# The issue order of four engines set by a table

## The chip, the core and the metric

The kernel runs on one core of one Trainium2 chip. The metric is device time in microseconds (us) from the start to the end of one execution. The core has TensorE (PE in the profile; PEld are its weight loads), VectorE (DVE), ScalarE (ACT), GpSimd (POOL) and SyncE (SP), each with its own queue of instructions, and 16 DMA engines. In this kernel SyncE does nothing but issue DMAs; its rows in the trace are named SPq.

## The reference

Linear attention with a random feature map, then two feed-forward layers. Batch 4, 8 heads, 576 positions, head dimension 64, 128 features; 2304 tokens of 512 elements go through the layers.

```python
def phi(x):
    proj = np.einsum('bhsd,md->bhsm', x, omega)
    sq = np.sum(x * x, axis=-1, keepdims=True) / 2.0
    h = proj - sq
    h = h - np.max(h, axis=-1, keepdims=True)
    return np.exp(h) / np.sqrt(m)
q_p, k_p = (phi(q_s), phi(k_s))
kv = np.einsum('bhsm,bhsd->bhmd', k_p, v)
z = np.sum(k_p, axis=2)
num = np.einsum('bhsm,bhmd->bhsd', q_p, kv)
den = np.einsum('bhsm,bhm->bhs', q_p, z)[..., None] + 1e-06
x = num / den                                  # then as (2304, 512)
h = x @ w_in                                   # 512 -> 2048
x = (h * (1.0 / (1.0 + np.exp(-1.702 * h)))) @ w_out
out = ((x @ w_a) * (x @ w_b)) @ w_out2         # 512 -> 1536 -> 512
```

Inputs are float32. The kernel works with pairs of float16, a high and a low part, so that each product takes three matmuls (high by high, high by low, low by high).

## The kernel before

**Stages.** The attention of batch 0 comes first (0 to about 57 us). Then the first feed-forward layer, ffn1, runs tile by tile, 512 tokens each, one tile for each batch and a rest tile of 256 tokens (L1134); beside ffn1 of one batch, the attention of the next batches is computed (batch 1 from 57 us on, batches 2 and 3 up to about 400 us). From about 500 us on ffn2 computes the second layer with a scheme of seven products for each block of 2x2 (`product`, L814 to L816 for a and b, `o_step`, L910 to L912 for the last matrix); its sums on VectorE are L835 (`total`), L841 (`times`), L864 and L868 (`ab_forms`), L918.

**Attention of one pair of heads** (`features`, in `kphase32` and `qphase`): load (`a_load`, L348, L352), high and low part (L403 on ScalarE, L404 on VectorE), a transpose by DMA (L409, xt), squares on ScalarE (L423, L431), the projection on TensorE (L415, L416), the maximum (L481), bias (L487), exponentials (L447), their parts (L457, L458), then for k the product with v (L529 to L531), for q a second DMA transpose (L575, eqT), products with kv (L585) and the division (L594 to L599). The result goes by a DMA transpose to xT (L635), in batch 0 by TensorE with the split L624.

**ffn1** (L655 to L692): for each of 16 blocks f of the hidden layer, h = w_in by xT on TensorE (L655 to L657), an activation on ScalarE (L664), th on VectorE (L667), gh on ScalarE (L676) and gl on VectorE (L677), then four accumulations y on TensorE (L690 to L692).

**Weights.** The weights come in 34 chunks of 1 MB (16 for w_in and w_out; then w_a0, w_b0, w_o2_0, w_a1, w_b1 and so on, two chunks each). Each is loaded as `wraw` (L201 in `w_load`, two buffers) and made into two float16 parts in `w_ops`: L215, L255 and L263 on VectorE assemble `wf` (128x1024 each), for the second layer L249 makes four sums `sx`, L273 on ScalarE gives the high part and L222 on VectorE the low part. A load i waits until L263 of chunk i-2 has read its buffer. `w_steps` takes so many steps of this generator at a point of the program, `w_need` as many as a use of the weights asks for.

**What sets the order.** The program is written as generators that are stepped in turn (`run`, `side_step`). The order of each engine's instructions comes from a scheduler that works while the program is built, with the order in which the program was written as a base. In five places a tie, `with tc.issue_after(x)`, keeps what is issued inside from going ahead of x: `fill` in ffn2 behind the last product (L971), the weight steps in `run` behind the last bias (L1077), the loads of v (L1090), the loads of k for the batch after (L1108) behind the transposed features of a q, and the first eight weight steps behind those of q0_2 (L1198).

Of the kernel before, what the change touches and what calls it, by code (L numbers as in the profile page):

```python
# [2 lines left out]

# [25 lines left out]
S_Y = 2.0**10  # L29
S_AB = 2.0**18  # L30
SILU = 3


@with_exitstack
def fused_kernel(
# [13 lines left out]
    nc = tc.nc  # L49
    B, H, S, D = q.shape  # L50
    M = omega.shape[0]
    DM, F1 = w_in_d.shape
    F2 = w_a_d.shape[1]
    P = 128
# [7 lines left out]
    T = 2 * NT + 1  # L62
# [5 lines left out]
    XSC = 1.0 / S_X  # L68
    DEN_EPS = 1e-6 * M / S_X

    mp = ctx.enter_context(tc.tile_pool(name="mp", bufs=4))
    stg = ctx.enter_context(tc.tile_pool(name="stg", bufs=2))
    ydram = ctx.enter_context(tc.tile_pool(name="ydram", bufs=1, space=bass.MemoryType.DRAM))
# [229 lines left out]
    own = {}  # L303
# [341 lines left out]
    def ffn1(j, xh, xl, n):  # L645
# [13 lines left out]
        def h_unit(f, cs=range(KC)):  # L659
            h_products(f, cs)  # L660
            ph = phs.pop(f)
            th = mp.tile([P, 512], F32, tag="f32", name=f"th{j}_{f}")
            if j < SILU:
                nc.scalar.activation(  # L664
# [67 lines left out]
    def y_load(j, n):  # L732
        yfs[j] = late["pool"].tile([P, KC, 512], F32, tag="yf", name=f"yf{j}", bufs=1)
        nc.sync.dma_start(out=yfs[j][:, :, :n], in_=ys[j][:, :, :n])
# [39 lines left out]
    def form_load(s, n):  # L774
        fo = form_tile(s)
        nc.sync.dma_start(out=fo[:, :, :, :, : n // 2], in_=stored[s % NT2])
# [15 lines left out]
    def ffn2():  # L792
# [8 lines left out]
        def product(k, m):  # L801
            g, j, n, nm = groups[k]
            b, a, r, fresh = PRODUCTS[m]
            if fresh:
                pool, tag = TAGS[b]
                banks[k, b] = pool.tile([P, 512], F32, tag=tag, name=f"p{nm}{b}{g}_{j}")
            o, w, fo = view(banks[k, b], n), w_ab[nm, g], forms[k // 2]
            h = n // 2
            for i in range(2):
                for c in range(2):  # L810
                    wh, wl = w[:, 0, i, a, c], w[:, 1, i, a, c]
                    xh, xl = fo[:, 0, r, c, :h], fo[:, 1, r, c, :h]
                    first, final = fresh and i == 0 and c == 0, i == 1 and c == 1
                    nc.tensor.matmul(o[:, i], wh, xh, start=first, stop=False, skip_group_check=True)  # L814
                    nc.tensor.matmul(o[:, i], wh, xl, start=False, stop=False, skip_group_check=True)  # L815
                    own["pe"] = nc.tensor.matmul(  # L816
                        o[:, i], wl, xh, start=False, stop=final, skip_group_check=True
                    ).ins
# [27 lines left out]
        def last(k):  # L846
            g, j, n, nm = groups[k]
            if nm == "a":
                nc.scalar.copy(sums[k][:, 3, :n], banks[k, "A"][:, :n])
                return  # L850
            times(k, slice(3, 4), banks[k, "A"][:, None, :n])
            side.append(ab_forms(k))
# [80 lines left out]
        def fill():  # L933
            if todo:
                o_step()
# [20 lines left out]
        def step(k, i):  # L956
            convert(k, i)
            step_side()
# [6 lines left out]
        for k, (g, j, n, nm) in enumerate(groups):  # L965
            s = k // 2
            if k:
                product(k - 1, 4)
                last(k - 1)
            if n < SM and nm == "a":  # L970
                with tc.issue_after(own["pe"]):  # L971
                    fill()
            if nm == "a" and s + 1 < NG * NT2:
                nj, nn = tiles[(s + 1) % NT2]
                if s + 1 < NT2:
                    y_load(nj, nn)
                else:
                    form_load(s + 1, nn)
            if nm == "b" and s + 1 < NT2:
                side.append(y_forms(*tiles[s + 1]))  # L980
            end = k == len(groups) - 1
            step(k, 0)
            product(k, 5)
            keep(k, 5)
            if nm == "b" and not end:
                fill()
            step(k, 1)
            product(k, 6)
            keep(k, 6)
            if nm == "b" and not end:  # L990
                fill()
            step(k, 2)
            product(k, 2)
            total(k, "B", 1, 0)
            if nm == "b":
                fill()
            step(k, 3)
            product(k, 3)
            total(k, "C", 6, 1)
            if nm == "b" and not end:  # L1000
                fill()
            step(k, 4)
            product(k, 7)
            total(k, "A", 5, 2)
            if nm == "b":
                times(k, slice(0, 3), sums[k][:, :, :n])
            if nm == "a" or j < B - 1:
                fill()
            step(k, 5)
            if nm == "a":  # L1010
                finish()
                fill()
            elif not end:
                while len(todo) > (j == B - 1):
                    o_step()
            begin(k + 1)
            if nm == "b":
                finish()
# [52 lines left out]
    def run(gen, rate, wmax):  # L1071

        due = 0.0
        for _ in gen:
            due += rate
            if rate < 1:
                with tc.issue_after(own["nb"]):  # L1077
                    w_steps(int(due), wmax)
            else:
                w_steps(int(due), wmax)  # L1080
            due -= int(due)
            side_step()
# [4 lines left out]

    def v_parts(b, behind):
        for part in range(NT):
            with tc.issue_after(behind.ins):  # L1090
                v_load(b, part)
            yield

# [8 lines left out]
    def begin_q(b, pool, xT, psp, t0, lag, f32):  # L1102
        for hp in range(NHP):
            def nx(hp=hp):
                if hp + 1 < NHP:
                    a_load(pool, "q", b, hp + 1)
                if b:
                    with tc.issue_after(own["xt", f"q{b}_{hp}"].ins):  # L1108
                        a_load(pool, "k", b + 1, hp)
                if hp + 1 == NHP:  # L1110
                    begin(b + 1, 0, v_parts(b + 1, own["xt", f"q{b}_{hp}"]))

            begin(b, t0 + lag * hp, qphase(pool, b, hp, xT, psp, nx, f32))
# [55 lines left out]
    with tc.tile_pool(name="att", bufs=2) as att:  # L1169
        own["om"] = att.tile([P, D], F32, tag="om", name="om", bufs=1)  # L1170
        nc.scalar.dma_start(out=own["om"], in_=omega)
        a_load(att, "k", 0, 0)
        a_load(att, "k", 0, 1, nc.scalar)
        zero = att.tile([P, 2, P], F16, tag="zero", name="zero", bufs=1)
        nc.vector.memset(zero, 0.0)
        for _ in range(10):
            nc.tensor.matmul(idle[:, 0:256], zero[:, 0], zero.rearrange("p a b -> p (a b)"), start=True, stop=True)
        warm = att.tile([P, 1], F32, tag="warm", name="warm", bufs=1)
        nc.vector.memset(warm, 0.0)
        nc.scalar.activation(out=warm, in_=warm, func=AF.Exp)  # L1180
        alloc_own(att)
        prep(att)
        fillers(5)
        for hp in range(2, NHP):
            a_load(att, "k", 0, hp)
        w_steps(START_W, NW1)
        begin_k(0, att, psp_start, 0, LAG, True)
        begin_q(0, att, xT, psp_start, NHP * LAG, LAG, True)
        for n in range(VT):
            side_step()  # L1190
        v_load(0)
        finish_side(0)
        fillers(FILL)
        w_load(0)
        w_load(1)
        for hp in range(NHP):
            a_load(att, "k", 1, hp)
        with tc.issue_after(own["xt", "q0_2"].ins):  # L1198
            w_steps(POST_W, NW1)
        following.append(ffn1(0, *xparts(xT), SM))  # L1200
        for b in range(1, B):
            x1 = x_tile(b, zp, "z")
            t0 = (0, 0, 1, -EARLY)[b]
            if b < 3:
                begin_k(b, att, psp_att, t0, AL, b == 1)
            begin_q(b, att, x1, psp_att, t0 + NHP * AL, AL, b == 1)
            if b == 2:
                begin_k(3, att, psp_att, 37 - EARLY, AL, False)
            ahead = next_tile(b, lambda: ffn1(b, *xparts(x1), SM))
            if b == 1:  # L1210
                run(head(following[0], 3), 1, NW1)
                run(following[0][0](first=3), 1, NW1)
                ahead()
            else:
                if b == 2:
                    run(head(following[-1], 3), 11 / 32, NW1 + 2)
                run(following[-1][0](ahead, 3 if b == 2 else 2), 11 / 32, (NW1 + 2, NWE)[b - 2])
# [11 lines left out]
    first.close()  # L1229
    late["sums"] = ctx.enter_context(tc.tile_pool(name="sums", bufs=1, side="right", reuse_waits="tile"))  # L1230
    ffn2()


# [34 lines left out]
```

## Time and profile before

| | |
|---|---|
| median of 3 runs | 897.08 us (896.01 to 898.03) |
| span of the profiled execution | 897.5 us |
| TensorE busy | 874.1 us (97%), weight loads 628.0 us |
| VectorE busy | 674.2 us (75%) |
| ScalarE busy | 457.6 us (51%) |
| instructions on TensorE, VectorE, ScalarE, GpSimd | 7094, 1212, 1088, 10 |
| DMA | 105.35 MB, 117 GB/s on average |

The page gives no time of the profiled execution apart from its span, from the first to the last instruction. That span is 0.4 us above the median. The rows below come from the trace of this execution; times are in us from its start.

### The profile page before, as it was taken

The numbers are of one execution on the slowest core, as the hardware profiler recorded it, in microseconds if no ns is written. First come the engines' busy times: TensorE is split into PE (matmuls) and PEld (weight loads), VectorE is DVE, ScalarE is ACT, GpSimd is POOL, SyncE is SP. The second block draws the span as 40 slices with busy tenths as digits, with TensorE's granted clock in tenths as the row PEclk, the third lists the DMA queues.
The fourth block names the chain that finished last, engine by engine and source line by source line (L and its number), as shares of the span: only waits on it lengthen the run. The fifth ranks groups of instructions, "written<-read, shape, count | busy, mean of one in ns | idle before, by whom it ended". The sixth has DMA issues, their size and how long they took to land.

```text
span 897.5 us, 17366 instructions
## 1 busy us (share of the span) xinstructions
PE 874.1 (97%) x7094; PEld 628.0 (70%) x7094; DVE 674.2 (75%) x1212; ACT 457.6 (51%) x1088; POOL 1.4 (0%) x10
## 2 busy tenths in 40 slices
PE   8999999999999999999999999999999999999997
PEld 6874655645554455444448888888888889888886
DVE  4889999787797787999611179987999557566766
ACT  6777875677656775564323354544443122233221
POOL 0000000000000000000000000000000000000000
PEclk8999999999999999999999999999999999999999
DMA  6945886344674314785401045232332022223312
GB/s 174 251 143 163 223 209 218 95 124 92 129 172 118 74 28 80 136 269 223 141 1 48 16 138 175 108 89 83 130 130 81 3 42 85 83 95 129 77 49 71
DMA packets 129343, 105.35 MB, mean 117 GB/s; under 512 B 97776, under 2 KB 111088, under 8 KB 127216
## 3 DMA queue, kind: packets, MB, share of 16 engines
q1 hardware_dynamic: 128558, 103.66, 41.0%
q8 instruction: 55, 0.90, 0.4%
q10 hardware_dynamic: 706, 0.59, 0.2%
q14 instruction: 24, 0.20, 0.1%
HBM read 71.07 MB, written 17.69 MB: 99 GB/s over the span
## 4 chain that ended last, share of the span: by engine, by line
PE 66%; DVE 17%; ACT 7%; DMA 4%; issue 2%; ACTq 0%; SPq 0%
PE y L690 4%; PE ph L655 4%; PE ph L656 4%; PE y L691 4%; PE ph L657 4%; PE y L692 4%; DMA xt_k<-x_k 3%; PE oA L912 2%; PE oA L910 2%; PE pbA L816 2%; PE pbA L814 2%; PE pbA L815 2%; PE oA L911 2%; PE pa L569 2%; PE paA L814 2%; PE paA L816 2%
## 5 line engine op out<-in xcount | busy, mean ns | idle before, releaser
L691 PE MATMUL y<-gl,w_out 128*128 128x512 f16 (+1 forms) x320 | 114.4, 358 | 0.6 <-DVE gl L677 0.4
L692 PE MATMUL y<-gh,w_out 128*128 128x512 f16 (+1 forms) x320 | 114.3, 358 | 0.0
L690 PE MATMUL y<-gh,w_out 128*128 128x512 f16 (+1 forms) x320 | 112.3, 358 | 0.7 <-ACT gh L676 0.7
L677 DVE SCALAR_TENSOR_TENSOR gl<-th,gh 128x512 f16<-128x512 f32 (+1 forms) x80 | 50.7, 635 | 66.6 <-ACT gh L676 66.3
L655 PE MATMUL ph<-xT,w_in 128*128 128x512 f16 x256 | 97.0, 379 | 1.5 <-DMA xT<-x_q_3x 0.7
L656 PE MATMUL ph<-xT,w_in 128*128 128x512 f16 x256 | 97.0, 379 | 0.3 <-DVE xT L624 0.3
L657 PE MATMUL ph<-xT,w_in 128*128 128x512 f16 x256 | 97.0, 379 | 0.0
L814 PE MATMUL paA<-forms,w_a 128*128 128x256 f16 (+1 forms) x240 | 61.0, 262 | 1.6 <-DVE ca L835 1.3
L814 PE MATMUL pbA<-forms,w_b 128*128 128x256 f16 (+1 forms) x240 | 61.0, 262 | 0.7 <-DVE cb L835 0.7
L816 PE MATMUL pbA<-forms,w_b 128*128 128x256 f16 (+1 forms) x240 | 61.0, 262 | 0.0
L815 PE MATMUL pbA<-forms,w_b 128*128 128x256 f16 (+1 forms) x240 | 61.0, 262 | 0.0
L816 PE MATMUL paA<-forms,w_a 128*128 128x256 f16 (+1 forms) x240 | 61.0, 262 | 0.0
L815 PE MATMUL paA<-forms,w_a 128*128 128x256 f16 (+1 forms) x240 | 61.0, 262 | 0.0
L912 PE MATMUL oA<-w_o,ab 128*128 128x256 f16 x216 | 58.9, 273 | 0.6 <-DVE ab L868 0.5
L910 PE MATMUL oA<-w_o,ab 128*128 128x256 f16 x216 | 58.9, 273 | 0.1
L911 PE MATMUL oA<-w_o,ab 128*128 128x256 f16 x216 | 58.9, 273 | 0.0
L676 ACT ACTIVATE gh<-th 128x512 f16<-128x512 f32 (+1 forms) x80 | 47.1, 589 | 23.0 <-DVE th L667 22.0
L824 ACT COPY ka<-paA 128x512 f32<-128x512 f32 (+1 forms) x30 | 16.3, 544 | 82.1 <-PE paA L816 82.1
L918 DVE SCALAR_TENSOR_TENSOR o<-oA,o 128x512 f32<-128x512 f32 (+1 forms) x45 | 28.4, 633 | 33.6 <-PE oA L912 33.6
L692 PEld LDWEIGHTS <-w_out 128*128 128x128 f16 x320 | 31.4, 98 | 29.3 <-issue 1.9
L657 PEld LDWEIGHTS <-w_in 128*128 128x128 f16 x320 | 31.5, 98 | 28.7 <-DVE w_in L222 1.1
L690 PEld LDWEIGHTS <-w_out 128*128 128x128 f16 x320 | 31.5, 99 | 28.6 <-issue 1.2
(211 smaller groups left out, 2373.8 us busy)
## 6 DMA issues: line engine op xcount, KB each, us to landing
wraw<-in_moe_w_out_dram SPq DMA_DIRECT2D x14, 1024.0 KB
forms<-fd SPq DMA_DIRECT2D x8, 1792.0 KB
wraw<-in_moe_w_in_dram SPq DMA_DIRECT2D x8, 1024.0 KB
fd<-forms SPq DMA_DIRECT2D x4, 1792.0 KB
wraw<-in_moe_w_a_dram SPq DMA_DIRECT2D x6, 1024.0 KB
wraw<-in_moe_w_b_dram SPq DMA_DIRECT2D x6, 1024.0 KB
vt<-in_v_dram SPq DMA_DIRECT2D x16, 256.0 KB
rawq<-in_q_dram SPq DMA_DIRECT2D x16, 256.0 KB
```

The source lines that it names most:

```text
L655: nc.tensor.matmul(ph[:, :n], w[:, 0, c, fs], xh(c), start=(c == 0), stop=False)
L656: nc.tensor.matmul(ph[:, :n], w[:, 0, c, fs], xl(c), start=False, stop=False)
L657: nc.tensor.matmul(ph[:, :n], w[:, 1, c, fs], xh(c), start=False, stop=(c == KC - 1))
L690: nc.tensor.matmul(o, w[:, 0, f % 4, cs], gh[f][:, :n], start=(f == 0), stop=False)
L691: nc.tensor.matmul(o, w[:, 0, f % 4, cs], gl[f][:, :n], start=False, stop=False)
L692: nc.tensor.matmul(o, w[:, 1, f % 4, cs], gh[f][:, :n], start=False, stop=(f == FC1 - 1))
L814: nc.tensor.matmul(o[:, i], wh, xh, start=first, stop=False, skip_group_check=True)
L815: nc.tensor.matmul(o[:, i], wh, xl, start=False, stop=False, skip_group_check=True)
L816: own["pe"] = nc.tensor.matmul(o[:, i], wl, xh, start=False, stop=final, skip_group_check=True).ins
L910: nc.tensor.matmul(bank[:, t], lh, wh, start=first, stop=False, skip_group_check=True)
L911: nc.tensor.matmul(bank[:, t], lh, wl, start=False, stop=False, skip_group_check=True)
L912: nc.tensor.matmul(bank[:, t], ll, wh, start=False, stop=final, skip_group_check=True)
```

## The change

The five ties become `contextlib.nullcontext`. At the end of the program a table is unpacked that holds, for each of four engines (TensorE, ScalarE, VectorE, SyncE), a permutation of that engine's instructions: 6870, 1019, 1212 and 224 numbers, each the place of an instruction in the order in which the program issues it. Between any two that follow one another in the table an edge is added without a semaphore (`NoSync`). The edges chain each engine's queue to one order. Instructions, operands, buffers and data dependencies remain as they are; GpSimd is not in the table.

Against the order of the kernel before, 1972 of TensorE's 6870 positions differ, 1687 of them between 50 and 400 us, by at most 90 places; 683 of ScalarE's, 841 of VectorE's (up to 254 places earlier, 45 later) and 120 of SyncE's.

```diff
+import contextlib
...
+ORDER = (
+    "eNqt3buua9uyGNZf2bjxCdjrRVKZASsXYMCJoMBwpMROBCeG/12ztyLn2ufeK8OBgz2x15ocfIxeg4tsVb3q//6X//Qf/+U//PWf"
...
+)
...
+    no_tie = contextlib.nullcontext
...
             if n < SM and nm == "a":
-                with tc.issue_after(own["pe"]):
+                with no_tie():
                     fill()
...
             if rate < 1:
-                with tc.issue_after(own["nb"]):
+                with no_tie():
                     w_steps(int(due), wmax)
...
         for part in range(NT):
-            with tc.issue_after(behind.ins):
+            with no_tie():
                 v_load(b, part)
...
                 if b:
-                    with tc.issue_after(own["xt", f"q{b}_{hp}"].ins):
+                    with no_tie():
                         a_load(pool, "k", b + 1, hp)
...
-        with tc.issue_after(own["xt", "q0_2"].ins):
+        with no_tie():
             w_steps(POST_W, NW1)
...
     ffn2()
+    import base64, json, zlib
+    nosync = mybir.DependencyInfo(mybir.DependencyClass.NoSync, mybir.DependencyReason.DATA)
+    for name, order in json.loads(zlib.decompress(base64.b64decode(ORDER))).items():
+        engine = getattr(mybir.EngineType, name)
+        ins = [i for i in nc.cur_bb.bb.instructions if i.engine == engine and type(i).__name__ != "BassTilePoolBoundary"]
+        assert len(ins) == len(order), (name, len(ins), len(order))
+        for a, b in zip(order, order[1:]):
+            tc.add_manual_dep(ins[b], ins[a].name, nosync, reason="order")
```

## Rows read from the trace of the kernel before

**Rows 1.** The page's engine line: busy us, share of the span, instructions
```profile
PE 874.1 (97%) x7094; PEld 628.0 (70%) x7094; DVE 674.2 (75%) x1212; ACT 457.6 (51%) x1088; POOL 1.4 (0%) x10
```

**Rows 2.** Windows: stretch, length, busy us of each engine, granted clock, DMA share, GB/s
```profile
57.00:82.00 25.00, 22.47 (x129) 11.18 (x129) 24.80 (x42) 17.02 (x64) 0.00 (x0) 1.00 0.57 163
82.00:160.00 78.00, 77.28 (x492) 44.06 (x490) 73.48 (x126) 55.04 (x203) 0.00 (x0) 1.00 0.73 199
160.00:258.70 98.70, 95.10 (x683) 51.99 (x682) 75.32 (x173) 68.82 (x173) 0.00 (x0) 1.00 0.51 115
258.70:300.00 41.30, 41.22 (x289) 20.45 (x288) 33.77 (x76) 27.54 (x61) 0.00 (x0) 1.00 0.67 154
300.00:400.00 100.00, 95.40 (x706) 48.23 (x704) 85.02 (x192) 66.42 (x158) 0.00 (x0) 1.00 0.50 111
400.00:500.00 100.00, 99.96 (x589) 57.58 (x589) 48.87 (x77) 36.64 (x67) 0.00 (x0) 1.00 0.28 100
500.00:893.00 393.00, 389.78 (x3787) 348.75 (x3784) 293.42 (x438) 144.83 (x243) 0.00 (x0) 1.00 0.27 89
```

**Rows 3.** Timeline of TensorE near 450 us: start, duration, instruction
```profile
450.33 0.38 PE L655 MATMUL ph<-xT,w_in 128*128 128x512 f16 x1
450.54 0.38 PE L656 MATMUL ph<-xT,w_in 128*128 128x512 f16 x1
```

**Rows 4.** Waits of TensorE, 57 to 160 us: waited us, times, longest
```profile
PE pa L415 <- ACT e_k L447: 1.8, 1, 1.8
```

**Rows 5.** Waits of TensorE, 160 to 300 us
```profile
PE pa L529 <- DVE sx L249: 1.0, 1, 1.0
PE y L690 <- ACT gh L676: 0.7, 1, 0.7
```

**Rows 6.** Waits of TensorE, 300 to 400 us
```profile
PE pa L415 <- DVE sx L249: 1.3, 1, 1.3
PE pa L585 <- DMA eqT_q<-e_q: 0.7, 1, 0.7
PE ph L655 <- DMA xT<-x_q_3x: 0.7, 1, 0.7
```

**Rows 7.** Waits of TensorE, 500 us to the end
```profile
PE paA L814 <- DVE ca L835: 1.3, 2, 0.8
PE pbA L814 <- DVE cb L835: 0.7, 1, 0.7
```

**Rows 8.** Timelines of VectorE and TensorE at 645 us; idle time before in brackets
```profile
645.15 1.22 DVE L255 SCALAR_TENSOR_TENSOR wf<-wraw,wf 128x1024 int32<-128x1024 int32 x1
646.28 0.68 DVE L835 TENSOR_TENSOR ca<-paA,ka 128x512 f32<-128x512 f32 x1
...
647.02 0.27 PE L814 MATMUL paA<-forms,w_a 128*128 128x256 f16 x1 [0.84 <-DVE ca L835]
```

**Rows 9.** The chain that ended last: start, us on the chain, DMA transposes
```profile
75.32 3.25 DMA xt_k<-x_k
...
85.78 6.70 DMA xt_k<-x_k
...
360.99 9.82 DMA eqT_q<-e_q
...
381.73 6.21 DMA xT<-x_q_3x
```

**Rows 10.** Timeline of SyncE's issues: the weight loads at 360 and 381 us
```profile
360.50 0.39 SPq L201 DMA_DIRECT2D wraw<-in_moe_w_out_dram  x1
...
381.13 0.37 SPq L201 DMA_DIRECT2D wraw<-in_moe_w_a_dram  x1
```

**Rows 11.** Windows of the tiles wf alone: busy us of VectorE and ScalarE
```profile
160.00:258.70 98.70, 8.10 (x12) 1.09 (x3) 1.00 0.51 115
258.70:400.00 141.30, 30.18 (x50) 5.75 (x12) 1.00 0.55 124
```

**Rows 12.** Groups of VectorE by line: busy us, mean ns, idle before
```profile
L263 DVE SCALAR_TENSOR_TENSOR wf<-wraw,wf 128x1024 int32<-128x1024 int32 x34 | 41.5, 1219 | 0.0
```

272 lines of the change are left out of this document (added).

## Prediction, made before the changed kernel was run

> **What bounds the kernel now.** I read the page's engine line first. TensorE is busy for 97% of the span, VectorE for 75%, ScalarE for 51% [rows 1]; by that alone only the 23 us that TensorE is idle could be had from a new order. The windows by stage come next [rows 2]: there the kernel falls into stages that an order can do very different things to. Until 57 us nothing differs in the table (its first TensorE position that differs is number 323 of 6870, at 62.9 us; VectorE's is 73, near 46 us). From 57 to 160 VectorE is busy 98.3 of 103 us. From 160 to 258.7 it has 23.4 us free while TensorE loses 3.6; from 300 to 400 TensorE loses 4.6; from 400 to 500 nothing; in ffn2, 500 to 893, 3.2. The clock is granted in full, 1.00, in all of these, so idle time is not paid for twice.
>
> Idle time in that view is too small, though. A 512-wide matmul has a record of 0.38 us but the next one starts 0.215 us later [rows 3], so the record of the last matmul before a stall covers the first 0.16 us of the stall. I went through the starts of all TensorE records and counted a stall wherever a start came over 0.1 us later than the usual spacing: 4 between 57 and 82, 12 up to 160, 19 up to 258.7, 4 up to 300, 22 up to 400, 21 in ffn2. Idle plus 0.16 for each is what can be won: 3.2, 2.6, 6.6, 0.7, 8.1 and 6.6 us, together 27.8. That is the ceiling from 57 us on. The Trainium skill (Perfetto Trace Analysis, "Identifying the Most-Contended Engine") says that matmul busy time is no good measure of how near TensorE is to its roofline, as matmuls are pipelined. The trace agrees in kind, by the two spacings above; by the busy share alone the sum below would have 14.8 us as its ceiling in place of 27.8.
>
> **What ends the stalls.** The waits of TensorE, stage by stage [rows 4 to 7]. The largest are not waits for arithmetic that is truly late; the releaser stood behind something else in its engine's queue. The pattern is plainest at 645: VectorE takes L255, 1.22 us of a weight conversion, at 645.15, the sum L835 that TensorE needs only at 646.28, and TensorE goes on at 647.02 after 0.84 us of idling [rows 8]. Two more in ffn2 are alike (0.4 and 0.7 us). From 300 to 400 the same holds for 1.3 us behind an L249 of a conversion, and for transposes by DMA: the chain of waits has 9.82 us for the transpose eqT at 360.99 and 6.21 for xT at 381.73, against 3.25 for one that nothing precedes [rows 9], and SyncE's issues show a weight load 0.5 and 0.6 us ahead of both [rows 10].
>
> **The change part by part.** The instructions are the same, and so are their data waits; the added edges are order on the same engine and cost no semaphore. So the sum is of stalls that go and stalls that come.
>
> *57 to 82 us.* The attention of batch 1 goes ahead of weight conversions and of ffn1's tile 0. Gain: the one long stall, 1.8 us of idling plus 0.16 [rows 4], because the transposed features are there some 8 us of TensorE work earlier. Cost: ScalarE's squares of rawk_1_1 and two VectorE steps now precede the split L624 that ends xT for tile 0, and VectorE, with 24.8 of 25.0 us busy, has no room to make that up; walking the queue by hand I have TensorE some 2 to 3 us later near 68 us. Taken together +0.5 us (bounds -2 to +3).
>
> *82 to 160.* VectorE busy 73.5 of 78 us before and no less work after; the stalls hold 2.6 us. I take 0 (bounds -1.5 to +1.5).
>
> *160 to 258.7.* This is where the work goes. Conversions of five chunks (wf17 to wf21: w_a0, w_b0 and w_o2_0) come forward from 258.7 to 400, where their chunk tiles alone take 30.2 us of VectorE against 8.1 here [rows 11]. For instance L263 of wf17 moves from position 437 of VectorE (260.1 us) to 287, between neighbours of 171 us, and wf20's from 667 (379.9 us) to 417. Adding up the durations of what stands ahead of each gl in both orders, VectorE has 12 us more in front of gl1_0 and 20 to 22 more in front of gl1_11. With 75.3 us of work it becomes 96 in 98.7. Gains: the conversions no longer lump, and some of the 6.6 us of stalls go. Costs: 15 steps of 1.22 us [rows 12] (L255, L263 and the wide L222 of five chunks), each of which can hold a th, gl or e that TensorE is waiting for. ScalarE gets the copies L273 of the same chunks, some 9 us on 68.8, and has room for them. The nearest rows for a full VectorE are the window before: from 82 to 160 it was 94% busy and TensorE lost 2.6 in 78 us, a smaller share than here at 76%. So fullness alone doesn't decide, and I take -1 (bounds -4, if two thirds of the stalls go, to +10, if each of the 15 costs 0.7 us).
>
> The Trainium skill (PSUM — Partial Sum Buffer, "Engine vs sequencer instructions") states that the queues of ScalarE and VectorE are strict FIFO. The row at 645 shows just that. It speaks against filling the gaps here: a conversion that is put in a gap that has closed by the time it is reached is not stepped around; by that rule at its worst the term is the +10 above.
>
> *SyncE.* Weight loads wraw18 to wraw23 (issued 198.0 to 388.7 before) come forward with their conversions, wraw19 ahead of a transpose of xT1 and wraw22 ahead of one of eqT_q2. A transpose right behind a load took 6.70 us where a free one took 3.25 [rows 9], so each such meeting costs up to 3.45 us if nobody has spare time. A load also waits for the L263 two chunks before it, and what stands behind it on SyncE waits too. I take 0 inside the -1 above, since two meetings (360 and 381 us) go and about as many come.
>
> *258.7 to 400.* VectorE loses some 21 us of work and the loads leave. I take away sx (1.3), eqT (0.7), xT (0.7) and 0.16 on top of each [rows 6], 3.2 us, and 1.3 of the other 5 us of small stalls: -4.5 (bounds -7 to +1, the latter if ScalarE's e_q, with 66 of 100 us busy, takes the place of VectorE).
>
> *ffn2, 500 to 893.* Conversions stand behind the sums L835, L864 and L868 ahead of which they stood; L263 of wf30 for example goes from 928 to 936, and L255 before the L835 at 646 goes behind it, so the sum is ready 1.13 us sooner and the 1.0 us stall is covered. The waits on VectorE's ca and cb are 2.0 us in three places, 2.5 with the hidden parts [rows 7]; ten smaller ones of 0.1 to 0.35 get 0.2 to 0.95 us of slack by the table, of these I take 1.5. The stalls in the tail after 880 us are unchanged. -4 (bounds -5.5 to -2); nothing here is full, VectorE 293 of 393 us, and I trust this term most.
>
> *The ties taken out* cost nothing by themselves: they set an order when the program is built, and the table sets it now.
>
> Sum: 0.5 + 0 - 1 - 4.5 - 4 = -9.0 us on a span of 897.5, that is 888.5 for an execution like the profiled one, which is 0.4 above the median of the runs; for the median **888.1 us**. What is 0.2% of it, 1.8 us, is about what a measurement of this kernel can tell from no change.
>
> **The rivals.**
> - *VectorE's queue turns against it (slower).* The place is 160 to 259 us, the price 15 wide conversions in VectorE's queue, each holding an operation that TensorE needs. The other terms give -8.0, so it decides from 0.53 us for each on; at 1.0 us the sum is +7: 904. For it: the order was laid out for exact durations, 96 of 98.7 us leave no room for a late DMA, and VectorE's delay holds SyncE's next load. Against: TensorE ran at a small loss with VectorE 94% busy just before. Chance 0.17.
> - *Loads in front of transposes (slower).* Four meetings at 3.45 us, none covered, make 13.8 - 8 = +5.8: 903. Decides from three on. For it, 9.82 us at 361; against, in before most transposes behind a load were covered by ffn1's work. Chance 0.05.
> - *Only ffn2 gains.* The middle trades stalls one for one: -4, 893. For it: the stalls from 300 to 400 have many releasers, ScalarE's e_q among them. Chance 0.20.
> - *The table fits nearly everywhere.* Two thirds of the 27.8 us go: 879. For it: work is now spread evenly over VectorE; against: nothing is gained before 160. Chance 0.12.
> - *It does not do what it says to the time.* What moves was waiting anyway, and the stalls are of data: 897. Against: the row at 645. Chance 0.07.
> - The forecast: 0.39.
>
> **How the numbers follow.** Faster holds the forecast, ffn2 alone and the good fit: 0.71, rounded to 0.70; the two slower rivals 0.22; 0.08 for the rest. The range must reach down to the good fit and up to about the middle of the slower cases, as 0.22 lie there: 877 to 903. The likeliest case by itself has its terms' bounds at about half their width: 882 to 895.
>
> **What the changed profile would show.** In the windows, VectorE near 96 us from 160 to 258.7 and near 98 (from 119) in the following 141; if TensorE's idle time in the former stays under 4 us, the first rival is out, and if it goes over 12 the rival holds. The waits for sx and for eqT between 300 and 400 should be gone, and the three waits for ca and cb in ffn2 too; the whole of ffn2 should last 4 us less. The stall of 1.8 us at 79 should be gone, with others near 60 to 70 in its place. I am wrong if VectorE's work lies as forecast and TensorE yet idles longer before 300 than it saves behind.

## The result and the profile after

The changed kernel takes 875.95 us (median of 4 runs, 875.21 to 876.83) against 896.82 us (896.01 to 898.03); the ratio is 0.9755 with an interval of 0.9715 to 0.9795. A second measurement beside other runs gave 875.86 us, 0.9757 (0.9738 to 0.9776). The sign was forecast; the gain is 20.9 us where 9.0 were, and the time is 1.05 us below the low end of the range.

The stretches that [rows 2] show of before, in the changed kernel (length, busy us of TensorE, its weight loads, VectorE, ScalarE, GpSimd, granted clock, DMA share, GB/s):

```profile
57.00:82.00 25.00, 22.50 (x142) 11.99 (x140) 24.62 (x43) 19.41 (x77) 0.00 (x0) 1.00 0.60 163
82.00:160.00 78.00, 77.26 (x496) 45.57 (x496) 76.02 (x128) 55.09 (x181) 0.00 (x0) 1.00 0.79 213
160.00:258.70 98.70, 98.35 (x699) 53.61 (x699) 93.68 (x208) 71.89 (x176) 0.00 (x0) 1.00 0.65 161
258.70:300.00 41.30, 41.30 (x309) 21.62 (x308) 32.80 (x78) 29.70 (x70) 0.00 (x0) 1.00 0.44 97
300.00:400.00 100.00, 99.87 (x722) 51.40 (x721) 81.76 (x175) 65.13 (x150) 0.00 (x0) 1.00 0.47 117
```

VectorE is fuller from 160 to 258.7 us by 18 us, 93.7 of 98.7, and TensorE idles 0.35 us there instead of 3.6; from 300 to 400 it idles 0.13 instead of 4.6. (The changed kernel is ahead by then, so the same window holds somewhat later work; the ledger below compares equal work.) What TensorE waited for (us in total, times, longest), 57 to 160, 160 to 300, and from 400 on, beside [rows 4 to 7]; between 300 and 400 the view is empty:

```profile
PE ph L933 <- DVE xT L901: 0.9, 1, 0.9
PE ph L932 <- ACT xT L900: 0.8, 1, 0.8
PE y L968 <- DVE gl L954: 0.7, 1, 0.7
...
PE ph L932 <- DVE th L944: 0.4, 1, 0.4
...
PE paA L1091 <- DVE ca L1112: 0.5, 1, 0.5
PE oA L1187 <- DVE o L1195: 0.3, 1, 0.3
```

The waits for sx, eqT and xT of [rows 5, 6] are gone and those of [rows 7] are down from 2.0 to 0.5 us. The chain that ended last (start, us) held the transposes of [rows 9], 3.3 to 9.8 us each, and three more; now no transpose is on it, and of the DMAs only two loads:

```profile
56.97 2.81 DMA rawk<-in_k_dram
116.37 6.23 DMA wraw<-in_moe_w_in_dram
```

**A ledger by stages.** Matmuls of ffn1 and ffn2 can be matched between the traces, so a stage can be timed from one matmul to the same one later. The marks are the first and the 66th L655, the 133rd and the 205th L690, the first L814 and the last L910; in before they start at 57, 178, 294, 410, 514 and 892 us. At the first four the same number of attention matmuls stands ahead in the changed kernel as in before, so the stages hold equal work. All lengths (us) are worked out from such starts:

| kernel | 57 to 178 | 178 to 294 | 294 to 410 | 410 to 514 | ffn2 |
|---|---|---|---|---|---|
| before | 120.8 | 115.9 | 116.4 | 104.2 | 378.0 |
| its order as a table (e1) | 121.3 | 116.9 | 115.9 | 104.2 | 378.0 |
| changed | 118.6 | 109.7 | 108.9 | 104.1 | 372.9 |
| TensorE's order alone (e2) | 184.1 | 146.0 | 123.1 | 104.1 | 377.8 |
| the others' alone (e3) | 179.8 | 159.3 | 117.4 | 104.2 | 375.8 |
| conversions left (e4) | 118.4 | 113.9 | 126.3 | 104.2 | 372.5 |
| ffn2 alone (e6) | 122.1 | 116.8 | 115.8 | 104.1 | 372.7 |
| to 160 alone (e7) | 119.5 | 116.5 | 115.9 | 104.2 | 378.0 |
| 160 to 455 alone (e8) | 128.4 | 109.3 | 108.9 | 104.2 | 378.0 |
| TensorE's stalls filled (e9) | 120.4 | 116.2 | 116.7 | 104.2 | 378.0 |
| TensorE's filling undone (e10) | 119.0 | 112.5 | 112.7 | 104.1 | 372.6 |
| conversions moved alone (e11) | 132.3 | 127.8 | 117.7 | 104.2 | 378.0 |
| changed to 284 us only (e12) | 118.9 | 109.6 | 113.7 | 104.2 | 378.0 |
| changed to 174 us only (e13) | 118.2 | 113.4 | 115.9 | 104.2 | 378.0 |

From before to changed: -2.1, -6.2, -7.5, -0.1 and -5.1 us. The traces also differ by 1.5 us ahead of the first mark. TensorE's order is the same up to there (VectorE's table differs from 46 us on), and executions with the order of before begin ffn1 anywhere from 54.1 (e1) to 57.1 us (before), so 1.5 us is within chance. The granted clock of the first 57 us is 0.94 in before, 0.97 in the changed kernel and 1.00 in e1, which fits.

### The profile page after: what moved, and what is told of

Same layout as the page of the kernel before. It is cut to its first block, busy times and chain, and to the rows that moved or that the text cites. A ratio compares the mean times of both kernels' runs of the same rounds, so it can differ in the third digit from the quotient of the medians.

```text
span 874.9 us, 17363 instructions
## 1 busy us (share of the span) xinstructions
PE 862.9 (99%) x7094; PEld 628.8 (72%) x7094; DVE 671.0 (77%) x1212; ACT 456.1 (52%) x1088; POOL 1.4 (0%) x10
## 4 chain that ended last, share of the span: by engine, by line
PE 81%; DVE 10%; ACT 3%; issue 1%; DMA 1%; SPq 0%; ACTq 0%; DVEq 0%
PE y L968 6%; PE y L967 6%; PE y L969 6%; PE ph L932 6%; PE ph L934 6%; PE ph L933 6%; PE oA L1187 3%; PE oA L1189 3%; PE oA L1188 3%; PE paA L1091 3%; PE pbA L1091 3%; PE paA L1092 3%; PE pbA L1092 3%; PE pbA L1093 3%; PE paA L1093 3%; DVE wf L540 2%
## 5 line engine op out<-in xcount | busy, mean ns | idle before, releaser
L934 PEld LDWEIGHTS <-w_in 128*128 128x128 f16 x320 | 31.3, 98 | 28.9 <-issue 1.2
L969 PEld LDWEIGHTS <-w_out 128*128 128x128 f16 x320 | 31.4, 98 | 28.8 <-issue 1.2
L933 PEld LDWEIGHTS <-w_in 128*128 128x128 f16 x320 | 31.4, 98 | 28.4 <-issue 1.4
```

The lines of the kernel that those rows point to most:

```text
L933: nc.tensor.matmul(ph[:, :n], w[:, 0, c, fs], xl(c), start=False, stop=False)
L934: nc.tensor.matmul(ph[:, :n], w[:, 1, c, fs], xh(c), start=False, stop=(c == KC - 1))
L969: nc.tensor.matmul(o, w[:, 1, f % 4, cs], gh[f][:, :n], start=False, stop=(f == FC1 - 1))
```

## The experiments

In the diffs `old[e]` and `new[e]` are the order of engine e in before and in the table, t_old and t_new the start of an instruction in the two traces. `near(t, keep=...)` is an order built by always taking, of the instructions whose inputs and buffers are there, the one with the smallest t, with the engines named in keep held to their order.

**The order of before as a table** (e1).

```diff
-ORDER = {e: new[e] for e in engines}
+ORDER = {e: old[e] for e in engines}
```

> The order of the kernel before, written out as a table for the four engines, with the five ties taken out. All theories: no change, 896.8 us within 0.2%, since a table edge costs no semaphore. Its profile also says how much of the 1.5 us by which the changed kernel is ahead when its orders first differ (at 57 us) is chance: if this one starts ffn1 anywhere from 55.5 to 57.1 us with the same order, the 1.5 us is not the table's.

Measured 897.68 against 898.31 us, 0.9990 (0.9976 to 1.0004). The edges and the absence of the ties cost nothing; ffn1 began at 54.1 us.

**TensorE's order without the others', and the others' without TensorE's** (e2, e3).

```diff
-ORDER = new
+ORDER = near(t_old, keep={"PE": new["PE"]})        # e2
+ORDER = near(t_new, keep={"PE": old["PE"]})        # e3
```

> TensorE's order from the new table; ScalarE, VectorE and SyncE in the order of before, save where the new order of TensorE forces a swap (231 of VectorE's 1212 places, by at most 15; 240 of ScalarE's, by at most 22). Theory A, the gain up to 400 us comes from TensorE's own queue, which now reaches each attention step when ScalarE has just freed its bank: at least 5 of the 7.7 us between 160 and 260 stay, with 3 from 300 to 400 and 1 to 2 in ffn2, so 884 to 888 us. Theory B, it comes from what stands ahead of the urgent steps in VectorE's and ScalarE's queues: at most 3 us in all, 894 us or more.

> The mirror image: TensorE in the order of before, the other three from the table save where TensorE's old order forces a swap (306 of VectorE's 1212 places, by at most 14). Theory A: little before 400 us, as TensorE still comes to each attention step too early; only ffn2's waits for sums go, 3 to 4 us: 891 to 894 us. Theory B: 880 us or less, with 160 to 260 free of stalls.

Measured 996.68 and 999.90 us, 1.108 (1.105 to 1.110) and 1.113 (1.109 to 1.117). Both theories fell: each half costs 100 us. Up to 30 us of each are the clock: TensorE was busy for 59 us in e2, and for 65 in e3, at a granted clock of 0.5 (1.2 GHz, the lower of its two levels), and half of that is what I estimate it lost at most. The rest is waiting. The waits of TensorE in e2 from 57 to 160 us and its window of 57 to 82 us:

```profile
PE pa L688 <- ACT e_k L720: 23.9, 5, 8.9
PE pa L688 <- ACT e_q L720: 3.4, 1, 3.4
```

```profile
57.00:82.00 25.00, 12.23 (x63) 5.84 (x61) 20.38 (x32) 12.74 (x40) 0.00 (x0) 0.76 0.46 126
```

TensorE comes to the attention steps that stood at 70 to 95 us in before 8 to 11 us of its work earlier, as in the table, but ScalarE and VectorE still have the old work in front of what these steps need. An order of one engine is only good or bad beside those of the others.

**The conversions left where they were** (e4).

```diff
-ORDER = new
+t = {i: t_old[i] + shift(i) if i in conversions(17, 23) else t_new[i]}   # 74 instructions
+ORDER = near(t)
```

> The whole table, but the conversions of chunks 17 to 23 and their loads stay where the kernel before had them relative to the work around (74 operations, 37 us of VectorE). Theory A: 160 to 260 keeps its 7.7 us; the stalls behind conversions and loads from 300 to 400 return in part (up to 3.5 us): 876 to 880 us. Theory C, the conversions' move into VectorE's free time is what won the middle: most of the 300 to 400 gain of 6.5 us goes and some of 160 to 260 with it, 883 us or more. The prediction's step, that the moved conversions cost TensorE about as much as the rest of the order gains in 160 to 260: then 160 to 260 is faster here than in the changed kernel.

Measured 897.57 us, 0.9987 (0.9972 to 1.0002): the whole gain is gone, yet not where any theory had it. Until the 118th L655 (263 us in before) this kernel is 11.0 us ahead of before, the changed one 10.9. So with VectorE at 75.2 of 98.7 us instead of 93.7 TensorE is no faster: **up to there the moved conversions cost nothing in the new order.** From there to 410 us it loses 14.7 us against before and 21.1 against the changed kernel; two stretches of 3.4 us each at clock 0.5, at 304 and 396 us, are at most 3.4 us of that. TensorE's waits, 260 to 420 us:

```profile
PE pa L689 <- ACT e_k L721: 3.4, 2, 2.2
PE y L965 <- DVE gl L951: 3.0, 3, 2.0
PE pa L859 <- DVE xf_q L873: 1.7, 3, 1.2
```

The new order has no room there for conversions. At the longest of these waits (it ends at 303.5 us) three sums `sx` of a conversion stand ahead of a bias on VectorE, and ScalarE's copy of the same conversion, 1.06 us, in the middle of the exponentials that TensorE waits for.

**Conversions moved alone** (e5, e11).

```diff
-ORDER = old
+t = {i: t_new[i] - shift(i) if i in conversions(17, 23) else t_old[i]}   # e5
+t = {i: t_new[i] - shift(i) if i in conversions(16, 23) else t_old[i]}   # e11, 87 instructions
+ORDER = near(t)
```

> The opposite of the run that left the conversions: the order of before, with only the conversions of chunks 17 to 23 and their loads at the places that the table gives them. If the move is worth its gain by itself: the stalls behind conversions and loads from 300 to 400 go (4 to 6 us) and 160 to 260 stays as before: 891 to 893 us. By the prediction's step and rival, that moved conversions hold urgent work in VectorE's queue: 160 to 260 loses 0.5 to 1 us for each of 15 wide ones, 8 to 15 us, and the sum is 899 to 907.

Measured 931.77 us, but as an experiment it failed: chunk 16 stayed behind, its buffers are those of the next, and the conversions came in one lump at 257 us that stopped TensorE for 19.1 us. Done again with chunk 16:

> The run with the conversions moved alone, done right: there chunk 16 had stayed behind, and as its buffers are chunk 17's, all later conversions came in one lump at 257 us. Here chunks 16 to 23 move together, each step to within 1 us of the table's place on the clock of before; all else is in the order of before. By the prediction's steps: 178 to 294 us of before costs up to 10 us more, 294 to 410 gains 3 to 4.5. Theory F, conversions that go into free time cost nothing and their absence from 294 to 410 is that stage's whole gain: 116 us unchanged in the first and 109 instead of 116.4 in the second, 889 us in all. Theory G, the move and the order of attention need each other: at most 2 us gained from 294 to 410, and 178 to 294 over 120 us.

Measured 922.96 us, 1.0274 (1.0245 to 1.0302). By its outcome this is theory G: against the mean of before and e1, 11 us are lost in each of the first two stages and 1.5 us in the third, where one wait of 3.5 us for a gl stands; without that about 2 us would have been won. But the loss of the first stage has another cause. All but 1.4 us of it comes after 162 us, behind one late load:

```profile
163.57 0.69 DVE L488 TENSOR_SCALAR wf<-wraw 128x1024 int32<-128x1024 int32 x1 [2.81 <-DMA wraw<-in_moe_w_a_dram]
166.69 0.94 ACT L546 ACTIVATE w_a<-wf 128x512 f16<-128x512 f32 x2 [5.41 <-DVE wf L536]
168.15 1.11 PE L835 MATMUL pa<-ident,e_q 128*128 128x128 f32 x4 [4.93 <-ACT eT_q L837]
```

VectorE waits for the load of a chunk of w_a, ScalarE's copy of that chunk waits for VectorE, and behind the copy in ScalarE's queue stands eT_q, which TensorE needs. TensorE idles 4.93 us, and from 166.5 us on the granted clock is 0.5 for 10.2 us, in which TensorE is busy for some 8.5; half of that is my estimate of what the clock cost. In the second stage the clock is 1.00 and neither VectorE nor ScalarE waits for a weight load: there it is the moved conversions. TensorE's waits from 185 to 315 us, and VectorE around one of them with TensorE's wait behind:

```profile
PE pa L688 <- ACT e_q L720: 4.0, 4, 1.8
PE pa L688 <- ACT e_k L720: 2.5, 4, 1.1
PE pa L802 <- ACT e_k L720: 2.4, 2, 1.3
PE pa L688 <- DVE kvl L778: 2.2, 2, 1.5
```

```profile
216.95 0.69 DVE L754 TENSOR_REDUCE mx_k<-pa 128x4 f32<-128x512 f32 x1 [1.08 <-PE pa L689]
217.56 1.22 DVE L528 SCALAR_TENSOR_TENSOR wf<-wraw,wf 128x1024 int32<-128x1024 int32 x1
218.71 0.66 DVE L940 SCALAR_TENSOR_TENSOR th<-th,ph 128x512 f32<-128x512 f32 x1
219.31 0.14 DVE L760 SCALAR_TENSOR_TENSOR mh_k<-mx_k,sq_k 128x4 f32<-128x4 f32 x1
...
219.97 0.15 DVE L760 SCALAR_TENSOR_TENSOR nb_k<-mh_k,sq_k 128x4 f32<-128x4 f32 x1
...
221.43 0.22 PE L802 MATMUL pa<-v_k,e_k 128*128 128x130 f16 x1 [1.26 <-ACT e_k L720]
```

Between the maximum and the bias stands a step of 1.22 us; the exponentials that free TensorE's bank wait for the bias. An attention step holds one of the two banks of `ps_att` from its last projection matmul to its last exponential; over the 26 steps of 178 to 294 us I measure 5.16 us on average in before and 6.00 here. As an estimate, 26 steps, 0.84 us longer, on two banks, is 10.9 us; the stage lost 11.4 (127.8 against 116.4). The Trainium skill (PSUM — Partial Sum Buffer, "Engine vs sequencer instructions") has VectorE's and ScalarE's queues as strictly first in, first out. These rows agree: the maximum was done at 217.64 us, and the step that takes it started at 219.31, behind the conversion and a th.

In the changed kernel the same steps hold their banks for 5.18 us on average, with conversions among them. That is as long as in before, and yet the stage is 6.2 us shorter, so the hold time is enough for the loss of e11, but not for the gain of the change. Its VectorE and TensorE around two wide steps:

```profile
224.52 1.22 DVE L499 SCALAR_TENSOR_TENSOR w_b<-sx,w_b 128x1024 f16<-128x1024 f32 x1
225.65 0.68 DVE L954 SCALAR_TENSOR_TENSOR gl<-th,gh 128x512 f16<-128x512 f32 x1
...
228.19 0.28 DVE L758 TENSOR_REDUCE mx_q<-pa 128x1 f32<-128x128 f32 x1
228.39 1.21 DVE L540 SCALAR_TENSOR_TENSOR wf<-wraw,wf 128x1024 int32<-128x1024 int32 x1
...
228.84 0.38 PE L968 MATMUL y<-gl,w_out 128*128 128x512 f16 x1
```

gl is done at 226.33 and used at 228.84, 2.5 us later. Of the 13 wide steps of chunks 17 to 21 between 160 and 262 us, one has right behind it what TensorE is waiting for (th at 182.07, after L499 at 180.93). Where a bias stands behind a wide step, less time is left than for that gl, as the exponentials come in between. One such step in the changed kernel, and the same exponentials and matmul in e4, which has this order without the conversions:

```profile
197.33 1.22 DVE L532 SCALAR_TENSOR_TENSOR wf<-wraw,wf 128x1024 int32<-128x1024 int32 x1
198.47 0.16 DVE L764 SCALAR_TENSOR_TENSOR nb_k<-mh_k,sq_k 128x5 f32<-128x5 f32 x1
198.66 1.40 ACT L724 ACTIVATE e_k<-pa,nb_k 128x128 f32<-128x128 f32 x5 [0.89 <-DVE nb_k L764]
200.00 0.22 PE L692 MATMUL pa<-om_h,xt_k 128*128 128x128 f16 x1
```

```profile
196.53 1.39 ACT L721 ACTIVATE e_k<-pa,nb_k 128x128 f32<-128x128 f32 x5
198.86 0.22 PE L689 MATMUL pa<-om_h,xt_k 128*128 128x128 f16 x1
```

In the changed kernel TensorE comes to the bank just as the exponentials end, straight from ffn1 and without a wait; in e4 they had ended 0.9 us before. From 178 to 294 us, 17 of the 21 attention matmuls in before that follow such exponentials start behind a stall, 5.7 us of stalls in all; in the changed kernel 2 of 19 do, 0.2 us, and in e11 17 of 21, 14.9 us. In the changed kernel none of them comes more than 0.2 us after its exponentials, in e4 some come up to 1.3 us after. So the banks come free no sooner than in before, but TensorE has ffn1 to do until then, and the conversions fill nearly all of the time that this leaves.

**Stages alone** (e6, e7, e8).

```diff
+ORDER = {e: [i in old[e] if t_old[i] < a] + [i in new[e] if a <= t_old[i] < z] + [i in old[e] if t_old[i] >= z]}
+a, z = 455, end    # e6
+a, z = 0, 160      # e7
+a, z = 160, 455    # e8
```

> The order of before up to 455 us, the table's from there on. The prediction's term for ffn2 is 4 us, the two traces show 5.3: 891.5 to 893 us against 897. If the terms of the stages don't add up (ffn2 gains only because it is entered in another state): under 2 us.

> The table's order for what ran before 160 us, the order of before for the rest. The prediction's terms: +0.5 us, 897.5; the two traces show 1.7 us won between 57 and 157: 895.3. The 1.5 us before 57 us are chance by the run with the old order as a table, which started ffn1 3 us early.

> The order of before up to 160 us and from 455 us on, the table's between. If the stages add up: 7.7 us from 160 to 260 and 6.4 from there to 400, 14 in all, 883 us. If the middle needs the earlier order (conversions of w_in and w_out end earlier, batch 1's attention is out of the way): half or less, over 889 us.

Measured 892.88 us (0.9956, 0.9942 to 0.9971), 895.58 (0.9987, 0.9977 to 0.9996) and 891.76 (0.9937, 0.9896 to 0.9979). ffn2 adds up. e8 shows both things in one kernel: from 178 to 410 us it has the changed kernel's lengths to 0.4 us, 14.1 us won, and it pays 7.6 us in the stage before, where the cut at 160 falls: the table's attention of batch 1 is ahead there, the old order's is not. Of the 7.6 us some 5 are the clock (half of 10.2 us, my estimate). It was granted at 0.5 for 3.4 us from 81.6 us on and for 6.8 us from 167.0 on, the latter behind three stalls of 0.5 to 1 us. Ten matmuls took 1.33 us ahead of that stretch, and twenty of the same kind 4.53 us in it:

```profile
162.49 1.33 PE L842 MATMUL pa<-kv,eT_q 128*128 128x65 f32 x10 [0.95 <-ACT e_q L720]
...
167.01 4.53 PE L842 MATMUL pa<-kv,eT_q 128*128 128x65 f32 x20 [0.36 <-ACT eT_q L837]
```

The five runs of e8 also follow their mean granted clock: 886.35 and 886.57 us at 0.999, 896.95 at 0.985.

**TensorE's stalls filled, and the filling undone** (e9, e10).

```diff
+for s in stalls(old["PE"], 160, 410):           # 38 places, 12.2 us
+    move(ceil(s.us / 0.216) ffn1 matmuls, ahead of s.step)     # e9, in old["PE"]
+    move(the same number, behind s.step)                       # e10, in new["PE"]
```

> The order of before on all engines, but at the 38 places between 160 and 410 us where TensorE stood over 0.1 us ahead of an attention step, so many ffn1 matmuls that follow anyway are put ahead of that step as the stall holds (65 matmuls moved, 12.2 us of stalls). Theory D, TensorE comes to attention steps too early by 0.1 to 1.5 us and the new order only fills that time: 9 to 12 us faster, 885 to 888 us, without moving a conversion. Theory E, the orders of the engines are a matched set and the early arrival is only where their sum shows: the stalls move to the next step, under 4 us, 893 us or more.

> The mirror image: the whole table, but TensorE's attention steps at the same 38 places stand so many ffn1 matmuls earlier as they stalled for in before (65 matmuls). Theory D: the 12.2 us of stalls return, 886 to 888 us against 876. Theory E: the new order has less to lose there, as conversions no longer stand behind: under 5 us, 881 us or less.

Measured 898.09 us (0.9999, 0.9984 to 1.0015) and 883.47 (0.9825, 0.9797 to 0.9853). Filling the old stalls wins nothing. In e9 the wait goes to others, 160 to 300 us:

```profile
PE pa L688 <- DVE kvl L778: 1.9, 4, 1.1
PE y L963 <- ACT gh L949: 0.7, 1, 0.7
```

As I read it, the step that TensorE does later is later for VectorE and ScalarE too, whose order has not changed. In the changed kernel the same 65 matmuls are worth 7.5 us, so TensorE's places are part of the gain, and only together with the other queues.

**The table up to a seamless cut** (e12, e13).

```diff
+ORDER = {e: [i in new[e] if t_new[i] < t] + [i in old[e] if t_new[i] >= t]}
+t = 283.9    # e12
+t = 174.3    # e13
```

> The table up to its 284 us, where attention and ffn1 stand to each other as in before (so without a seam), then the order of before, with the conversions up to chunk 21 already done. Theory F: the 116 us from there to 410 become 109 by the absence of conversions alone; ffn2 as before: 881 us. Theory G: that stage stays within 2 us of before, 114 to 117 us: 887 us or more.

> The table up to its 174 us, where attention and ffn1 again stand to each other as in before, then the order of before; chunks 16 and 17 are converted early. 57 to 178 us of before should take the table's 118.6 instead of 120.8. Theory F: 178 to 294 gains what two conversions less are worth there (the stall of 1.2 us behind the sums of chunk 17), 294 to 410 nothing: 893 us. Theory G: 178 to 294 within 0.5 us of before: 895 us.

Measured 886.08 us (0.9864, 0.9835 to 0.9894) and 891.34 (0.9927, 0.9902 to 0.9951). With the conversions up to chunk 21 done and the old order behind, 294 to 410 us takes 113.7: of the 7.2 us that the stage wins (108.9 against 116.1, the mean of before and e1) the absence of these conversions and their loads is 2.4 and the order 4.8. That division holds from the old order's side alone: in the new order the same conversions cost 17.4 us there (e4, 126.3 against 108.9). Waits of e12, 284 to 403 us:

```profile
PE pa L689 <- ACT e_k L721: 1.6, 2, 0.9
PE pa L803 <- ACT e_q L721: 0.4, 2, 0.2
```

Neither F nor G is right alone. In e13, 178 to 294 us wins 3 us with two chunks less to convert in it and the old order for the rest; 294 to 410 wins nothing.

**What stays in the changed kernel** (e14, with e15, the changed kernel beside it).

```diff
+before_(ACT, xT at 58.12, the square at 57.08); before_(ACT, 4 exponentials at 78.83, the square at 77.85)
+before_(DVE, xT at 59.30, mx at 58.02); before_(DVE, mh and gl at 127.91, wf at 126.70)
+before_(DVE, th at 182.07, w_a at 180.93); before_(DVE, ca at 554.48, ab at 553.88)
```

> The table with nine VectorE and ScalarE instructions moved by at most four places, each ahead of the one that held it where the changed kernel's trace still shows TensorE waiting: the high and the low part of xT (0.79 and 0.89 us at 58), one gl behind a wide conversion step (0.74 at 128), one th behind another (0.35 at 182), one sum ca (0.47 at 554) and four exponentials behind four squares (0.34 at 79). If what is left is still what stands ahead in a queue: about 3 of these 3.6 us (with 0.16 hidden in each) go, 873 us against 876. If the chain of attention only passes the delay on: within 1 us of the table.

> The changed kernel itself, beside the run with nine instructions moved, for a comparison on one chip: 875 to 877 us.

Ten instructions moved, not nine: the mh in front of the gl went with it. Measured 876.04 us (0.9758, 0.9742 to 0.9774) beside 875.86 (0.9757, 0.9738 to 0.9776). The two waits after 160 us that were aimed at are gone (ffn2 takes 372.2 instead of 372.6), those before are replaced, 50 to 160 us:

```profile
PE pa L896 <- DVE xf_q L873: 1.0, 1, 1.0
PE ph L929 <- ACT w_in L547: 0.8, 1, 0.8
PE pa L689 <- ACT eT_q L838: 0.7, 1, 0.7
```

In the changed kernel VectorE is busy 100.6 of the 103 us from 57 to 160 us, which fits: what is put first there holds something else.

## Why the prediction was right and wrong

- **What bounds the kernel: right.** The gain is of TensorE's stalls. Counted as in the prediction, from 57 us on, 27.5 us of stalls over 0.1 us were there and 7.3 are left: three quarters are gone. This is the rival "the table fits nearly everywhere", at 0.12, which put it at two thirds and 879 us.
- **57 to 160 us, +0.5 forecast, -1.2 (-0.4 to -2.1) measured by e7** (-2.1 in the traces, up to 178 us). The long stall of [rows 4] went and two of 0.8 and 0.9 us at 58 came, for the reason given: squares ahead of xT on ScalarE, then VectorE. Up to 68 us TensorE lost 2.8 us by stalls instead of 1.0, which is near the 2 to 3 us expected, and over 57 to 82 us the stalls are 3.3 us instead of 3.2. I had nothing for 82 to 160, where they fell from 2.6 to 1.2 us.
- **160 to 258.7 us, -1 forecast, -6.2 measured (178 to 294 in the ledger): the step that failed.** VectorE took on the work as forecast (96 said, 93.7 seen), but 0 to 0.7 us for each of 15 wide steps was the wrong kind of price. In the old order the moved conversions cost 11.4 us in this stage (e11), a little over the upper bound; in the new one nothing (e4 beside the changed kernel), and of the 6.6 us of stalls counted from 160 to 258.7 us, all that could be won, 0.7 are left; from 178 to 294 us, 5.5 us of those that went stood ahead of attention matmuls that wait for the exponentials. A step's price is not its own: it is what stands behind it and how soon TensorE needs that. Both orders were at hand, and I priced the move by the old one's neighbours. What should have been read is, for each moved step, the few instructions behind it in the new table and the distance to the matmul that takes them, through the exponentials where it is a bias. By the prediction's own test (idle under 4 us there) the first rival is out.
- **258.7 to 400 us, -4.5 forecast, -7.5 measured (294 to 410).** The stalls named did go. But of the gain only 2.4 us are the absence of conversions by itself (e12); the other 4.8 need the new order among attention and ffn1, of which the prediction had nothing. I took the releaser's name (sx, eqT) for the cause.
- **ffn2, -4 forecast, -5.1 in the traces, 3.9 by the medians of e6: right**, and independent of the rest. The sum of [rows 8] now stands ahead of the conversion, as said.
- **SyncE, 0: right** as far as it shows; no transpose is on the chain any more. **Ties, 0: right** (e1).
- **The median.** The profiled execution stood further above the others than I took it to: a run's time is 1.9 us above its span where both are known (876.83 beside 874.9), so the profiled execution of before was some 2 us slow; it also began ffn1 latest of all, at 57.1 us. That adds to the difference of the traces, not of the medians.

The separate terms were the deeper fault. I summed edits as if each had its worth; e2, e3, e9 and e11 show that parts of this change cost 98, 102, 0 and 24 us alone (of the 24 some 10 by a late load and the clock), and the whole wins 21. Stages nearly do add up: 1.2 us (e7), 14.1 from 178 to 410 us (e8) and 3.9 (e6) make 19.2. Engines, and kinds of instructions, do not. What stays open is which queue's order won the 6.2 us of 178 to 294: TensorE takes ffn1 ahead of attention there by 3 to 9 us of its work (matched starts of 200 to 280 us), undoing the small part that filled the old stalls gives back 2.9, filling the old order's stalls in the same way wins nothing (e9), and no run separates the rest from VectorE's and ScalarE's order, or takes SyncE's order by itself.

## What to carry to other kernels

When a change reorders queues that work in order, price each moved step in the new order: look at what stands behind it there and how long before its use by the bottleneck that is done, through the engines in between. An engine's busy share says little about that: beside VectorE at 95% TensorE idled 0.35 us, and beside VectorE at 76% 3.6 us. Change the queues that feed each other together; half a good schedule can be far worse than a poor whole one.

## What was not expected of the hardware

A change of order alone moves this kernel from 876 to 1000 us with the same instructions, and where the granted clock fell behind stalls (e2, e8, e11) they cost more than their length. Where TensorE stood idle half the time (e2, 57 to 82 us, 12.2 of 25 us busy) the granted clock was 0.76 on average, between its two levels of 1.2 and 2.4 GHz; in before and in the changed kernel it is 1.00 in the same stretch, at 22.5 us busy. From 57 us on the clock stayed at 1.00 in before and in the changed kernel until the last 2 us, so nothing that the ledger shows as won there is the clock's; of what e2, e3, e4, e8 and e11 lost, a part is.
